# A one-token transformer block over a long key/value cache: four value slots per matmul, tiles ordered by head group, weights in longer runs and the MLP weights last

## The chip, the cores and the metric

The kernel runs on one core of one Trainium2 chip. The metric is the time of one execution on the device in microseconds (us); the number given for a kernel is the median of several executions. A profile of one execution stands beside it. It has the span, that is the time from the first to the last event on the core, and every instruction and every transfer with its start and its duration.

A core has five engines that run their own instruction streams and wait for each other with semaphores: PE (TensorE, matrix multiplication; the load of the stationary operand is shown separately as PEld), DVE (VectorE), ACT (ScalarE), POOL (GpSimd) and SP (SyncE, which here only issues transfers). Sixteen DMA engines move data from the chip's memory (HBM) to the on-chip memory (SBUF). The PE accumulates in PSUM.

## What is computed

Four batch rows, one new token each, width D = 512. With `mod = silu(c) @ w_mod` cut into six parts of width 512 (sa, ca, ga, sb, cb, gb):

```python
h = _layernorm(x) * (1 + ca) + sa
x = x + ga * attention(h)          # 32 heads, 4096 cached keys, 128 per head
h = _layernorm(x) * (1 + cb) + sb
x = x + gb * mlp(h)
```

The attention multiplies h by wq (512 x 4096), scores the query of each head against that head's 4096 cached keys, takes the softmax, sums the 4096 cached values with these weights, and multiplies the 4096 results by wo (4096 x 512). The cache is read, not written: 4 x 32 x 4096 x 128 bf16 numbers each for keys and values, 134.2 MB each. The MLP is a gated one: `z = gelu(h @ w_in)` (512 x 1792), its second half is normalised, scaled by a scalar w_sp and shifted by a scalar b_sp, multiplied with the first half, and multiplied by w_out (896 x 512). With one token per row, each cached number is used once, so there is no reuse for a matrix engine to gain from.

## The kernel before, in words

**Tiles.** The work is cut into NT = 32 tiles. A tile is one batch row and four heads: 4 x 4096 keys, laid out as 128 partitions x 128 slots x 128 numbers (partition p holds 128 consecutive key positions of head p // 32). So K of a tile is one 4 MB transfer in which each partition receives one run of 32 KB, and V likewise. Tile i is batch row i // 8 and head group i % 8.

**Buffers and order of transfers.** Two buffers for K (`kt`) and two for V (`vt`). All large transfers are issued by SP, in program order, and SP waits at each for its buffer to come free. Order: the first 1 MB of w_mod (`wmA`, L94), wq (L96), K of tiles 0 and 1, V of tile 0, the other 2 MB of w_mod (`wmB`, L123). Then in iteration i: K of tile i + 2 (L109) when the PE has finished with K of tile i, and V of tile i (L117) when the PE has finished with V of tile i - 2. In iteration 2 wo is loaded (L448) into the room that wq and w_mod leave, in iteration 4 w_in and w_out (L451, L453). V of the last tile (31) is cut into four pieces of 64, 32, 16 and 16 slots (`TAIL`). It has to wait for the V buffer that tile 29 uses.

**One iteration** (loop over i, from `QPLAN` on; the order on each engine is the order written there, nothing reorders it). For tile i: DVE multiplies K in place by the queries in two halves (`mult`, L276); the PE adds up the products over d with identity matmuls (`reduce_d`, L282, 16 per half); DVE adds the last eight (`sum8`, L291). For tile i - 1: the row maxima on DVE and the exponentials on ACT, which are written into a 128 x 128 x 4 tile `pbd` that has one nonzero column in each block of four (`scores`, L300 to L314), and the sums (`norm_r`, `norm_a`). For tile i - 2: the value product (`pv`, L340): one matmul for each of the 128 slots, with the 128 x 4 block of `pbd` as stationary operand and the 128 x 128 values of the slot as moving operand. The four column groups of the array (`tile_position`) take the slots in turn, into a PSUM tile of 128 x 128. ACT copies it out (`o_out`, L347). For tile i - 3: a matmul that adds the four groups and turns the result (`o_cols`, L352), the division by the sum (`o_scale`), and the product with the 4 x 128 rows of wo of this head group, 16 matmuls (`o_proj`, L366), which DVE adds to the accumulator (`o_add`, L374). Part of the MLP's first product, that of the sb term, is done in iteration 6 (`zbp`, L459).

**The end**, after the loop: `scores` of tile 31; `pv`, `o_cols` and `o_proj` of tile 30; the second layer norm for all rows without tile 31; then for tile 31 a value product the other way round, 128 matmuls with V as stationary operand (L537), so that the pieces can be used as they land; `o_scale`, `o_proj`, a correction of the layer norm for the last batch row; w_in (56 matmuls, L561), gelu, w_out (two times 28 matmuls, L603) and the output.

Of the kernel before, what the change touches and what calls it, by code (L numbers as in the profile page):

```python
# [8 lines left out]
BF16 = mybir.dt.bfloat16  # L9
# [6 lines left out]
HQ = 4  # L16
# [6 lines left out]
def kernel(  # L23
# [16 lines left out]

# [12 lines left out]
    R = P // HQ  # L55
    assert DH == P and R == 32 and NJ % KC == 0 and KC * RD == 512 and sum(TAIL) == NJ
    att_scale = float(DH) ** -0.5
    LN_EPS = 1e-5
    GC = 2.0 * 0.7978845608028654
# [14 lines left out]
    def ps_q():  # L74
# [8 lines left out]
    wsp_t = consts.tile([P, 1], BF16, name="wsp_t")  # L83
    bsp_t = consts.tile([P, 1], BF16, name="bsp_t")
    nc.gpsimd.dma_start(out=wsp_t, in_=B_w_sp[0:1, 0:1].to_broadcast((P, 1)))
    nc.gpsimd.dma_start(
        out=bsp_t, in_=B_b_sp.rearrange("(a b) -> a b", b=1).to_broadcast((P, 1))
    )
# [3 lines left out]
    wmod_v = w_mod.rearrange("(j p) n -> p j n", p=P)  # L92
    wmA = pre.tile([P, DJ, 2 * D], BF16, name="wmA")
    nc.sync.dma_start(out=wmA, in_=wmod_v[:, :, 0:2 * D])  # L94
    wq_sb = pre.tile([P, DJ, H * DH], BF16, name="wq_sb")
    nc.sync.dma_start(out=wq_sb, in_=A_wq.rearrange("(j p) n -> p j n", p=P))  # L96
    wmB = pre.tile([P, DJ, 4 * D], BF16, name="wmB")

    def kv_view(cache, i):
        b, g = divmod(i, NQ)  # L100
        v = cache[b, g * HQ:(g + 1) * HQ].rearrange("h s d -> (h s) d")
        return v.rearrange("(p n) d -> p n d", p=P)

    kts, vts = {}, {}

    def load_k(i):
        if i < NT:
            kts[i] = kvp.tile([P, NJ, DH], BF16, name="kt", bufs=2)
            nc.sync.dma_start(out=kts[i], in_=kv_view(A_k_cache, i))  # L109

    def load_v(i):
        if i < NT:
            vts[i] = kvp.tile([P, NJ, DH], BF16, name="vt", bufs=2)
            v = kv_view(A_v_cache, i)
            n0 = 0
            for n in TAIL if i == NT - 1 else (NJ,):
                nc.sync.dma_start(out=vts[i][:, n0:n0 + n, :], in_=v[:, n0:n0 + n, :])  # L117
                n0 += n
# [4 lines left out]
    nc.sync.dma_start(out=wmB, in_=wmod_v[:, :, 2 * D:6 * D])  # L123

# [7 lines left out]
    eps = consts.tile([P, 1], F32, name="eps")  # L132
    nc.vector.memset(eps, LN_EPS)
# [3 lines left out]
    nc.vector.memset(inv_f, 1.0 / FH)  # L137
    st2 = consts.tile([P, 2, DJ + 1], F32, name="st2")
# [7 lines left out]
    for q in range(HQ):  # L146
        nc.vector.memset(mask4[R * q:R * (q + 1), q:q + 1], 1.0)
    sel4 = consts.tile([P, HQ], F32, name="sel4")
    nc.vector.tensor_reduce(
# [523 lines left out]
```

## Time and profile before

| | |
|---|---|
| median of 3 executions | 687.23 us (686.74 to 687.46) |
| profiled execution: own time | 686.22 us |
| profiled execution: span | 684.4 us |
| read from HBM | 282.73 MB, 413 GB/s over the span |
| PE busy | 402.3 us (59%), 6574 matmuls and 6574 weight loads |
| DVE busy | 376.3 us (55%) |
| ACT busy | 93.4 us (14%) |
| mean granted PE clock | 0.805 of full |
| packets of the transfers | 16955, of these 6272 under 2 KB |

The counts of packets by size in the page include the smaller ones: 6272 under 2 KB are 1272 under 512 B and 5000 above. Bytes on the transfer queues are given in the page by queue: q1 is the hardware queue of SP's transfers, q8 carries instructions.

A profile is read from the whole to the part: first which resource is busy all the time (the table of 40 slices), then the chain of waits that ends last, then single groups of instructions and what ended the idle time ahead of them, then the timeline at the two ends of the program, where the steady pattern does not hold.

### The profile page before, as it was taken

How to read it: one execution, taken by the hardware profiler on the slowest of the kernel's cores; microseconds unless marked ns; L12 is line 12 of the kernel's file. 1: busy time of each engine (PE TensorE's matmuls, PEld its weight loads, DVE VectorE, ACT ScalarE, POOL GpSimd, SP SyncE). 2: the span in 40 equal slices, each digit the busy share in tenths (PEclk: the TensorE clock that was granted, in tenths of full speed). 3: DMA queues.
4: the chain of work that ended last, by engine and by line, in shares of the span. 5: the costliest groups of instructions: out<-in, count | busy, mean ns of one | idle time of the engine just before them, and what ended most of it. 6: DMA issues, size and time to landing. Idle time of an engine off the chain costs nothing.

```text
span 684.4 us, 14205 instructions
## 1 busy us (share of the span) xinstructions
PE 402.3 (59%) x6574; PEld 229.5 (34%) x6574; DVE 376.3 (55%) x486; ACT 93.4 (14%) x310; POOL 4.5 (1%) x17
## 2 busy tenths in 40 slices
PE   2193854844765545566745556765555566655565
PEld 2142523523332223333313333332233333323345
DVE  3383582761566645555665555556655554666542
ACT  1020211110111110111111101111110011111112
POOL 2000000000000000000000000000000000000000
PEclk9997875978788877788877887788887787788895
DMA  8999999999999999999999999999999999999971
GB/s 338 428 426 428 425 415 420 439 409 435 435 436 425 428 434 426 430 432 434 432 430 431 429 430 427 428 429 430 428 429 432 430 427 436 432 428 426 435 309 60
DMA packets 16955, 283.64 MB, mean 414 GB/s; under 512 B 1272, under 2 KB 6272, under 8 KB 8064
## 3 DMA queue, kind: packets, MB, share of 16 engines
q1 hardware_dynamic: 16800, 282.73, 96.9%
q8 instruction: 51, 0.84, 0.5%
q14 instruction: 8, 0.07, 0.0%
q0 software_dynamic: 64, 0.00, 0.0%
q10 hardware_dynamic: 32, 0.01, 0.0%
HBM read 282.73 MB, written 0.00 MB: 413 GB/s over the span
## 4 chain that ended last, share of the span: by engine, by line
DMA 60%; DVE 20%; PE 18%; SPq 1%; issue 0%; ACT 0%; DVEq 0%
DMA kt<-in_A_k_cache_dram 59%; DVE kt L276 17%; PE red L282 16%; DMA vt<-in_A_v_cache_dram 2%; DVE S L291 1%; PE ops L340 1%; PE qps L261 0%; DVE mrow L300 0%; SPq L117 0%; DVE mt L304 0%; DVE nM L306 0%; DVE mb L302 0%; PE qps L561 0%; DVE nM L307 0%; PE sm L486 0%
## 5 line engine op out<-in xcount | busy, mean ns | idle before, releaser
L282 PE MATMUL red<-kt,ident_bf 128*128 128x512 bf16 x1024 | 293.5, 451 | 235.6 <-DVE kt L276 235.5
L276 DVE TENSOR_TENSOR kt<-kt,qbc 128x8192 bf16<-128x8192 bf16 x64 | 282.9, 4421 | 236.1 <-DMA kt<-in_A_k_cache_dram 236.1
L282 PEld LDWEIGHTS <-ident_bf 128*128 128x128 bf16 x1024 | 116.4, 114 | 393.9 <-issue 228.4
L314 ACT ACTIVATE pbd<-S,nM 32x128 bf16<-32x128 f32 x128 | 73.8, 577 | 255.1 <-DVE nM L307 253.5
L340 PE MATMUL ops<-vt,pbd 128*4 128x128 bf16 x3968 | 63.4, 222 | 3.3 <-issue 3.3
L340 PEld LDWEIGHTS <-pbd 128*4 128x4 bf16 x3968 | 56.6, 86 | 4.8 <-issue 4.2
L291 DVE TENSOR_REDUCE S<-red 128x64 f32<-128x512 f32 x64 | 43.7, 683 | 4.0 <-PE red L282 3.9
L347 ACT COPY osb<-ops 128x128 f32<-128x128 f32 x31 | 8.2, 265 | 263.7 <-PE ops L340 263.7
L314 ACT ACTIVATION_READ_ACCUMULATOR pbd<-S,nM 32x1 f32 x128 | 32.1, 251 | 0.0
L366 PE MATMUL sm<-oTs,wo_sb 128*128 128x1 bf16 x512 | 17.3, 163 | 15.2 <-DMA wo_sb<-in_A_wo_dram 14.7
L366 PEld LDWEIGHTS <-wo_sb 128*128 128x128 bf16 x512 | 17.9, 101 | 15.4 <-DMA wo_sb<-in_A_wo_dram 14.7
L329 PEld LDWEIGHTS sm<-rsb,ones_f 128*128 128x128 f32 x64 | 12.1, 190 | 6.8 <-DVE acc L374 2.3
L352 PEld LDWEIGHTS sm<-sel,osb 128*128 128x128 f32 x62 | 11.6, 190 | 5.4 <-ACT osb L347 1.2
L261 PE MATMUL qps<-wq_sb,hTb 128*32 128x128 bf16 x512 | 9.4, 231 | 5.8 <-DMA wq_sb<-in_A_wq_dram 5.1
L374 DVE TENSOR_TENSOR acc<-acc,sm 128x4 f32<-128x4 f32 x31 | 4.2, 135 | 12.7 <-PE sm L366 12.7
L266 ACT CAST qbc<-qps 128x512 bf16<-128x512 f32 x8 | 4.7, 585 | 46.3 <-PE qps L261 46.3
L261 PEld LDWEIGHTS <-hTb 128*32 128x32 bf16 x512 | 8.1, 103 | 7.6 <-issue 6.6
L329 PE MATMUL sm<-rsb,ones_f 128*128 128x4 f32 x64 | 9.1, 212 | 2.3 <-DVE acc L374 2.3
L357 DVE TENSOR_TENSOR oTs<-sm,rz 128x4 bf16<-128x4 f32 x32 | 5.1, 158 | 8.8 <-PE sm L352 4.3
L322 DVE TENSOR_SCALAR rsb<-mask,rs 128x4 f32<-128x4 f32 x32 | 7.2, 224 | 4.9 <-ACT pbd L314 4.9
L300 DVE TENSOR_REDUCE mrow<-S 128x1 f32<-128x128 f32 x32 | 9.2, 286 | 1.1
L352 PE MATMUL sm<-sel,osb 128*128 128x4 f32 x62 | 8.9, 214 | 0.9 <-ACT osb L347 0.9
(132 smaller groups left out, 91.2 us busy)
## 6 DMA issues: line engine op xcount, KB each, us to landing
kt<-in_A_k_cache_dram SPq DMA_DIRECT2D x32, 4096.0 KB
vt<-in_A_v_cache_dram SPq DMA_DIRECT2D x31, 4096.0 KB, 31.9
wq_sb<-in_A_wq_dram SPq DMA_DIRECT2D x1, 4096.0 KB
wo_sb<-in_A_wo_dram SPq DMA_DIRECT2D x1, 4096.0 KB
wmB<-in_w_mod_dram SPq DMA_DIRECT2D x1, 2048.0 KB, 49.1
vt<-in_A_v_cache_dram SPq DMA_DIRECT2D x1, 2048.0 KB, 8.5
win_sb<-in_B_w_in_dram SPq DMA_DIRECT2D x1, 1792.0 KB
wmA<-in_w_mod_dram SPq DMA_DIRECT2D x1, 1024.0 KB, 5.4
```

Of the source, the lines that this page charges most:

```text
L261: nc.tensor.matmul(qp[R * q:R * (q + 1), gi, :], lhsT=hTb[:, k, b, :], rhs=wq_sb[:, k, h * DH:(h + 1) * DH], start=(k == 0), stop=(k == DJ ...
L276: nc.vector.tensor_tensor(out=kt, in0=kt, in1=bc(qbc[:, i, :], KC), op=ALU.mult)
L282: nc.tensor.matmul(red, lhsT=ident_bf, rhs=kt[:, :, m * RD:(m + 1) * RD], start=(m == 0), stop=(m == DH // RD - 1),)
L291: nc.vector.tensor_reduce(out=st[i, "S"][:, kc * KC:(kc + 1) * KC], in_=st.pop((i, "red", kc)), axis=AX.X, op=ALU.add,)
L300: nc.vector.tensor_reduce(out=mrow, in_=S, axis=AX.X, op=ALU.max)
L314: nc.scalar.activation(out=pbd[r, :, q], in_=S[r, :], func=AF.Exp, bias=nM[r, :], scale=att_scale, accum_out=rs[r, :],)
L322: nc.vector.tensor_scalar(out=rsb, in0=mask4, scalar1=st.pop((i, "rs")), scalar2=None, op0=ALU.mult)
L329: nc.tensor.matmul(z, lhsT=ones_f, rhs=st.pop((i, "rsb")), start=True, stop=True)
L340: nc.tensor.matmul(opss[i % 2][g:g + HQ, :], lhsT=pbds[i % 3][:, n, :], rhs=vts[i][:, n, :], start=(n < 4), stop=(n >= NJ - 4), tile_posit ...
L347: nc.scalar.copy(out=osb, in_=opss[i % 2])
L352: nc.tensor.matmul(op, lhsT=st.pop((i, "osb")), rhs=sel4, start=True, stop=True)
L366: nc.tensor.matmul(wp[:, j:j + 1], lhsT=wo_sb[:, g * HQ + q, j * P:(j + 1) * P], rhs=oT[:, q:q + 1], start=(q == 0), stop=(q == HQ - 1),)
```

## The change

1. **Values.** `pv` takes four slots per matmul: 32 matmuls per tile with a 128 x 16 block of `pbd` as stationary operand and 4 x 128 = 512 values as moving operand. The PSUM tile becomes 128 x 512, and only the blocks where the slot of the weights equals the slot of the values are wanted. DVE picks them with four operations and the mask `selg` (`o_pick`), in place of ACT's copy; it does so one iteration later than ACT did.
2. **Order of tiles.** Tile i is head group i // 4 and batch row i % 4. After four tiles a head group is complete, and `o_proj` runs once per group with four columns (16 matmuls per four tiles). The last group is done in two parts, three rows and one.
3. **Weights in longer runs.** w_mod is loaded whole (3 MB) as the first transfer, one run of 24 KB per partition; wq in one run of 32 KB per partition, w_in in one of 14 KB; wo of the first seven groups in runs of 2 KB. A partition now holds other rows of a matrix than before, so columns are taken with a step of four (`j:D:DJ`), also where they are loaded as stationary operand. `queries` uses 16 matmuls of 512 columns where there were 64 of 128.
4. **MLP weights last.** w_in and w_out are issued in iteration 30, behind V of tile 31, not in iteration 4. The sb term is no longer computed ahead; it rides as four further columns in the w_in product.
5. **Last tile.** V of tile 31 goes into a K buffer, the one that K of tile 30 leaves, and is issued in iteration 30. K of tile 31 is loaded in two halves.
6. Small things: w_sp and b_sp come in by two 2-byte transfers in iteration 2 in place of two broadcast ones at the start; the first layer norm uses one matmul where it used four; the turn of x at the end uses 16 small matmuls in place of four and is read from PSUM in place of through ACT; the last additions are ordered otherwise.

```diff
-    wmA = pre.tile([P, DJ, 2 * D], BF16, name="wmA")
-    nc.sync.dma_start(out=wmA, in_=wmod_v[:, :, 0:2 * D])
+    wm_sb = pre.tile([P, DJ, 6 * D], BF16, name="wm_sb")
+    nc.sync.dma_start(out=wm_sb, in_=w_mod.rearrange("(p j) n -> p j n", p=P))
...
-    nc.sync.dma_start(out=wq_sb, in_=A_wq.rearrange("(j p) n -> p j n", p=P))
+    nc.sync.dma_start(out=wq_sb, in_=A_wq.rearrange("(p j) n -> p j n", p=P))
...
-        b, g = divmod(i, NQ)
+        g, b = divmod(i, B)
...
-            nc.sync.dma_start(out=kts[i], in_=kv_view(A_k_cache, i))
+            load(kts[i], kv_view(A_k_cache, i), (KC, NJ - KC) if i == L else (NJ,))
...
+        vts[i] = kvp.tile([P, NJ, DH], BF16, name="kt" if i == L else "vt", bufs=2)
+        load(vts[i], kv_view(A_v_cache, i), TAIL if i == L else (NJ,))
...
-    nc.sync.dma_start(out=wmB, in_=wmod_v[:, :, 2 * D:6 * D])
...
-        for n in range(n0, n1):
-            g = R * (n % 4)
+        for m in range(NJ // G):
+            n = slice(m * G, (m + 1) * G)
+            g = R * (m % 4)
             nc.tensor.matmul(
-                opss[i % 2][g:g + HQ, :], lhsT=pbds[i % 3][:, n, :], rhs=vts[i][:, n, :],
-                start=(n < 4), stop=(n >= NJ - 4), tile_position=(0, g),
+                opss[i % 2][g:g + G * HQ], lhsT=pbds[i % 3][:, n, :], rhs=vts[i][:, n, :],
+                start=(m < 4), stop=(m >= NJ // G - 4), tile_position=(0, g),
             )
...
-        nc.scalar.copy(out=osb, in_=opss[i % 2])
+        nc.vector.tensor_scalar(
+            out=osb, in0=ops[:, 0, :], scalar1=selg[:, 0:1], scalar2=None, op0=ALU.mult
+        )
+        for g in range(1, G):
+            nc.vector.scalar_tensor_tensor(
+                out=osb, in0=ops[:, g, :], scalar=selg[:, g:g + 1], in1=osb,
+                op0=ALU.mult, op1=ALU.add,
+            )
...
-                    wp[:, j:j + 1], lhsT=wo_sb[:, g * HQ + q, j * P:(j + 1) * P],
-                    rhs=oT[:, q:q + 1], start=(q == 0), stop=(q == HQ - 1),
+                    wp[:, j, :], lhsT=w[:, j:D:DJ], rhs=oTs[:, g * B + b0:g * B + b1, r, t],
+                    start=(q == 0), stop=(q == HQ - 1),
...
-        elif i >= 2:
+        elif 2 <= i < L:
             load_v(i)
...
-            nc.sync.dma_start(out=wo_sb, in_=A_wo.rearrange("(j p) n -> p j n", p=P))
+            nc.sync.dma_start(
+                out=wo_sb, in_=A_wo[0:hl].rearrange("(t p r) n -> p t r n", p=P, r=2)
+            )
+            nc.sync.dma_start(out=wo_last, in_=A_wo[hl:H * DH].rearrange("(q p) n -> p q n", p=P))
-        if i == 4:
...
+        if i == L - 1:
+            load_v(L)
             win_sb = wts.tile([P, DJ, F], BF16, name="win_sb")
-            nc.sync.dma_start(out=win_sb, in_=B_w_in.rearrange("(j p) n -> p j n", p=P))
+            nc.sync.dma_start(out=win_sb, in_=B_w_in.rearrange("(p j) n -> p j n", p=P))
             wout_sb = wts.tile([P, NH, D], BF16, name="wout_sb")
             nc.sync.dma_start(out=wout_sb, in_=B_w_out.rearrange("(j p) n -> p j n", p=P))
-        if i == 6:
...
```

## The prediction, made before the changed kernel ran

> **What bounds the kernel now.** I read the 40 slices first, then the transfer queues, then the chain that ended last.
>
> ```profile
> DMA  8999999999999999999999999999999999999971
> GB/s 338 428 426 428 425 415 420 439 409 435 435 436 425 428 434 426 430 432 434 432 430 431 429 430 427 428 429 430 428 429 432 430 427 436 432 428 426 435 309 60
> DMA packets 16955, 283.64 MB, mean 414 GB/s; under 512 B 1272, under 2 KB 6272, under 8 KB 8064
> ...
> q1 hardware_dynamic: 16800, 282.73, 96.9%
> q8 instruction: 51, 0.84, 0.5%
> ...
> DMA kt<-in_A_k_cache_dram 59%; DVE kt L276 17%; PE red L282 16%; DMA vt<-in_A_v_cache_dram 2%; DVE S L291 1%; PE ops L340 1%; PE qps L261 0%; DVE mrow L300 0%; SPq L117 0%; DVE mt L304 0%; DVE nM L306 0%; DVE mb L302 0%; PE qps L561 0%; DVE nM L307 0%; PE sm L486 0%
> ```
>
> The transfers are at 9 tenths from the second slice to the 38th, at some 430 GB/s. The chain names DVE and PE too, but it only follows a K buffer round: a K transfer issued at 616.43 landed 24.6 us later, of which 9.7 us are its own 4.19 MB at 430 GB/s; the other 15 us are queue ahead of it. So a tile's compute may be some 15 us later before a transfer starts late. In the loop DVE (55% busy) and PE (59%) have room; what counts is the bytes, the rate, the head and the end. The stretches show the end:
>
> ```profile
> 101.00:112.00 11.00, 0.00 (x0) 0.00 (x0) 0.00 (x0) 0.00 (x0) 0.00 (x0) 0.50 1.13 413
> ...
> 600.00:640.00 40.00, 23.41 (x360) 12.89 (x360) 22.69 (x26) 5.16 (x18) 0.00 (x0) 0.83 1.00 430
> ...
> 650.00:661.00 11.00, 7.61 (x172) 5.07 (x171) 5.73 (x20) 2.56 (x9) 0.00 (x0) 1.00 0.65 263
> 661.00:672.00 11.00, 7.87 (x289) 7.25 (x290) 1.99 (x12) 0.77 (x3) 0.00 (x0) 0.74 0.79 326
> ```
>
> The last two numbers of a row are the DMA share and GB/s. From 650 to 661 us a third of the transfer time is empty. The timeline says why:
>
> ```profile
> 641.05 4.43 DVE L276 TENSOR_TENSOR kt<-kt,qbc 128x8192 bf16<-128x8192 bf16 x1 [8.09 <-DMA kt<-in_A_k_cache_dram]
> ...
> 655.85 1.96 PE L340 MATMUL ops<-vt,pbd 128*4 128x128 bf16 x128
> ...
> 657.85 3.11 SPq L117 DMA_DIRECT2D vt<-in_A_v_cache_dram  x4
> ...
> 661.59 1.96 PE L340 MATMUL ops<-vt,pbd 128*4 128x128 bf16 x128
> ...
> 671.74 0.59 PE L537 MATMUL sm<-pbd,vt 128*128 128x4 bf16 x16 [0.66 <-DMA vt<-in_A_v_cache_dram]
> ...
> 674.92 1.64 PE L561 MATMUL qps<-hc,win_sb 128*128 128x4 bf16 x56 [0.53 <-DVE hc L554]
> ...
> 678.31 0.94 PE L603 MATMUL red<-wout_sb,z1w 128*32 128x128 bf16 x28
> ```
>
> K31 has landed at 641.05 (call this T). V31 is issued only at 657.85, when the value product of tile 29 has freed its buffer; its last piece lands at 671.7, and 12.7 us of serial work follow.
>
> **Why not all engines run dry at 650.** In the trace's packet records each transfer ends with 16 small packets, one per DMA engine. Around K31 three engines end at 640.2 to 640.3, the other 13 at 632.0 to 635.7. A transfer counts when its slowest engine is done, so three engines, some 8 us behind, set T. What puts them behind: each of the 51 q8 packets is followed by a hole. The engine's 32 KB packets otherwise follow each other every 1.214 us; at a q8 packet there is about 1.05 us of nothing and the next packet takes about 0.5 us longer, 1.5 us together. And I take q8 for PE's instructions: its 0.84 MB over PE's 6574 + 6574 instructions is 64 B each, 256 to a packet, and the other engines run a few hundred each. An engine 8 us behind has had about five more of these than the others.
>
> **The change, part by part, up to T.** Packet times on one engine, medians of the records: 32 KB 1.214 us, 8 KB 0.309, 4 KB 0.159, 3.5 KB 0.140, 2 KB 0.086, 1 KB 0.046. That is 27 bytes per ns for the long and 22 for the 1 KB ones.
> - *MLP weights behind V31:* 512 x 0.140/16 + 896 x 0.046/16 = 4.5 + 2.6 = **7.05 us** less ahead of T (by bytes at 430 GB/s, 6.4).
> - *Head.* Before, w_mod's first part and wq were in at 17.3 and K0 at 28.4, and wmB came later: 512 x 0.159/16 = 5.1; in all 33.5. After: first bytes at 2.3 (the 2 to 3 us stretch moves 133 GB/s), w_mod 128 x 0.91/16 = 7.3, wq and K0 9.7 each, 0.8 to land: 29.8. **-3.6 us.** Of that some 1.5 is the hole from 6 to 7 us (74 GB/s) between the first two transfers; if it stays, -2.1. Next late would be K2's issue: K0's landing plus the same 15.4 us as before (28.37 to 43.72) is 45.2; the queue holds K1 and V0 until 48.7, and an issue takes about 1.6 us to the first byte (0.74 to 2.3). Covered by 2 us; if not, up to 2 us of loss.
> - *wo:* 4096 x 0.046/16 = 11.8 becomes 1792 x 0.086/16 + 512 x 0.046/16 = 11.1: **-0.7** (0 to -1.4). *K31 in halves:* 16 KB packets took 0.623, so 8 x (1.246 - 1.214) = **+0.25**.
> - *Fewer PE instructions.* Matmuls and loads: `pv` falls from 256 to 64 per tile (31 tiles: -5952), `queries` from 1024 to 256, `o_proj` from 1024 to 288, `zb` by 112; `o_cols` and the last turn of x add some 400. 13148 becomes about 6000, so 51 packets become 23. If each engine's share shrinks alike, the three engines' 7.6 us that I count ahead of T as lag (K0 to K31 and V0 to V28, 61 x 9.71 = 592.3, weights at the packet times 36.6, start and first hole 3.8: 632.7; seen 640.3) become 3.3: **-4.3 us**. Nothing in this trace shows a run with fewer: bounds 0 and -6.5 (the lag all but one hole).
> - *DVE.* `o_pick` per tile: one operation like L634 on a 128x128 PSUM tile (0.29) and three like L631 (0.36) = 1.4 us, and a reciprocal more; ACT's copy (0.27) goes. DVE does 11.3 us per 20 us now, so 12.6 after: hidden by the 15 us of queue. The same holds for `pv`: 32 x 512 columns are the 128 x 128 columns of before; 1.96 us if the four column groups overlap as now.
>
> A page rule speaks against the longer runs. The Trainium skill, "DMA: Bandwidth & Descriptors", section Specifications, gives 512 B as the minimum transfer for line rate, by which 1 KB runs would already be at full rate and the wo term would be 0 and the head term only the hole. The rows above differ from it: 0.046 us per 1 KB, and the stretch 101 to 112, which is wo, has a DMA share of 1.13 and 413 GB/s.
>
> T becomes 641.05 - 7.05 - 3.6 - 0.7 + 0.25 - 4.3 = **625.7**.
>
> **From T to the end.** V31 no longer waits: its buffer is free when `reduce_d` of tile 30 ends (635.8 before, earlier than V30's issue at 638.3), so V29, V30, V31, w_in, w_out follow T without a hole: V30 at T + 19.5 = 645.2, V31 at 655.2 (its small pieces make it 10.0), w_in 659.6, w_out 662.2, each plus up to 1. Compute: scores of tile 31 were done 19.8 us after T before (660.6), where the PE's last K product took to 655.4; with the first half of K31 landing 4.9 us early they are done near T + 13, ahead of V30. So V30 starts the last chain. Before, `pv` of tile 30 to the first of the 128 tile-31 matmuls took 661.59 to 667.76 = 6.2. After: +1.1 for `o_pick` in place of the copy; +1.0 for `pv` at a slower clock (the PE has idled about 6 us; L282 shows 6.28 against 3.61 us for the same 16 matmuls, so 1.96 to 3.9; I take 3.0); +0.4 for 16 weight loads with a step of four (no such row; between the 34 ns apart of L366 and the 114 ns of L282's loads, 0 to 1.3; I take nearer to L366, the same product). 8.7: 653.9. The 128 matmuls take 3.9 (3.33 for 112): 657.8, V31 is in by then. To w_in, 672.33 to 674.92 = 2.6, plus 0.4: 660.8, w_in just in. From there 9.5 to the end as before, less 0.6, because two of the six last DVE operations no longer wait for the variance: **669.7**; w_out is used 3.4 us after w_in starts, at 664.2, and landed by 663.2.
>
> The Trainium skill, "SBUF — State Buffer", section "Door 1: The DMA port swizzle", has bf16 strides up to 8 elements free, so the 0.4 twice would be 0 by it and the end 668.9; no run here shows it yet.
>
> Span 684.4 - 669.7 = 14.7 less. The profiled execution took 686.22; 671.5 then. The median was 1.0 above the profiled one, which I add: **672.5 us**.
>
> **Rivals.**
> 1. *The instruction packets are not what holds the three engines back*, or the holes move to others: without the 4.3, 676.8; and with the first hole staying, 678.3. For it: I infer engines from phases, and the records do not name them. Against: a hole at each q8 packet.
> 2. *The tail's new work costs more* (PE cold, weights with steps several times slower, V30 late): +0.9 on `pv`, twice 0.9 on loads, 1.0 on V30: 672.5 + 3.7 = 676; with the first part of 1 also, 680.
> 3. *Slower: the four column groups stop overlapping* with 512 columns. Place: `pv`, 32 matmuls per tile at L282's 0.226 (3.61/16) to 0.39 (6.28/16) each: 7.2 to 12.5 us instead of 1.96. PE is busy 60.5 per 100 us, 11.8 per tile of 19.5; less 1.96 plus 12.5 is 22.3, above 19.5, and 31 tiles times 2.8 give about +87, 760. It decides from a `pv` of 9.6 us per tile. At 7.2 the loop hides it and the two last passes cost 10: 683, still within or under the present. Against: 128 matmuls of 219 ns each end within 1.96 us, and the positions 0, 32, 64, 96 stay.
> 4. *It does not do what it says:* w_out and the last part of wo still run in 1 KB pieces and wo in 2 KB, so little of "long runs" is there to gain; that is in the sum. If the other order of tiles reads HBM worse, 2% of 430 GB/s (13 us) would eat the gain. K and V alternate now from far apart without a dip.
>
> **Chances.** Forecast 0.58 (669 to 675.5), rival 1 0.22, rival 2 0.12, the mild form of 3 0.03, slower or the same (3 in full, or 4) 0.05, of which 0.02 within 0.2%. A difference under 0.2% (1.4 us) is about what a measurement of this kernel can't tell from none. The range is from all terms at their good end (fetches -6.5, loads 0, `pv` 1.96: 668) to rivals 1 and 2 together: 668 to 680.
>
> **What would show it.** q8 near 23 packets; no empty stretch ahead of the last transfer; K31's landing near 626 (with fetches not mattering, near 630); the last matmuls of tile 31 waiting for PE's own chain, not for V31; `pv` near 2 us per tile. Wrong if `pv` takes over 7 us, if SP issues K2 after the queue has run out near 49 us, or if the loop's rate is under 425 GB/s.

## The result, and the profile after

| | before | after |
|---|---|---|
| median | 687.34 us (686.74 to 687.46) | 675.48 us (675.37 to 675.57) |
| profiled execution: own time, span | 686.22, 684.4 us | 675.57, 673.8 us |
| mean rate over the span | 413 GB/s | 420 GB/s |
| PE matmuls, weight loads | 6574, 6574 | 2971, 2971 |
| DVE busy | 376.3 us | 422.9 us |
| K31 landed | 641.05 us | 629.2 us |

The ratio of the times is 0.9829 (95% interval 0.9809 to 0.9848). One further execution, of 1869 us, is left out of the range and of the ratio (without it the median is 675.38). The forecast was 672.5 with a range of 668 to 680: 3.0 us too low, inside the range.

The page of the kernel after: the 40 slices, the counts of packets, the transfer queues, the chain that ended last.

```profile
DMA  9999999999999999999999999999999999999993
GB/s 374 436 431 432 407 414 418 432 434 427 429 430 433 434 433 432 427 428 431 433 430 432 431 435 428 424 434 433 430 429 432 433 435 426 431 432 424 433 414 132
DMA packets 13556, 283.19 MB, mean 420 GB/s; under 512 B 1228, under 2 KB 2644, under 8 KB 4692
...
q1 hardware_dynamic: 13488, 282.73, 98.2%
q8 instruction: 23, 0.38, 0.2%
...
DMA kt<-in_A_k_cache_dram 53%; DVE kt L275 21%; PE red L281 12%; DVE osb L362 3%; DVE S L290 1%; PE ops L350 1%; DVE osb L358 1%; DVE mrow L299 1%; DVE mt L303 1%; PE sm L387 1%; DVE rz L341 1%; DVE nM L305 0%; DVE mb L301 0%; PE qps L261 0
```

The bytes are the same (282.73 MB), the rate in the loop is the same (some 430 GB/s), and the kernel is still bound by K transfers. What differs: the first slice starts faster, the 39th is nearly full (414 GB/s where it was 309), and q8 carries 23 packets where it carried 51.

The groups of the value product: `pv` on the PE before (L340) and after (L350), and the four operations of `o_pick` on DVE (busy time, then the mean of one in ns).

```profile
L340 PE MATMUL ops<-vt,pbd 128*4 128x128 bf16 x3968 | 63.4, 222 | 3.3 <-issue 3.3
...
L350 PE MATMUL ops<-vt,pbd 128*16 128x512 bf16 x992 | 60.7, 387 | 0.0
...
L362 DVE SCALAR_TENSOR_TENSOR osb<-ops,selg,osb 128x128 f32<-128x128 f32 x93 | 32.6, 351 | 3.3
...
L358 DVE TENSOR_SCALAR osb<-ops,selg 128x128 f32<-128x128 f32 x31 | 10.8, 349 | 4.0 <-PE ops L350 3.4
```

992 matmuls keep the PE busy for 60.7 us; 3968 kept it busy for 63.4 before. The mean of one went from 222 to 387 ns with four times the columns, so the four column groups still overlap. `o_pick` is 0.35 + 3 x 0.35 = 1.4 us per tile.

The stretches of the kernel after. Behind the length of a stretch stand the busy time of PE, PEld, DVE, ACT and POOL, each with its number of instructions, then the granted PE clock (1.00 is full), the DMA share and GB/s.

```profile
200.00:600.00 400.00, 247.65 (x1575) 106.95 (x1576) 266.14 (x359) 48.54 (x168) 0.00 (x0) 0.81 1.00 431
600.00:640.00 40.00, 26.15 (x177) 11.74 (x176) 28.80 (x37) 4.63 (x16) 0.00 (x0) 0.87 1.01 431
640.00:650.00 10.00, 5.74 (x58) 3.00 (x60) 3.68 (x14) 2.30 (x8) 0.00 (x0) 0.83 0.98 419
650.00:661.00 11.00, 7.36 (x148) 5.33 (x141) 3.05 (x14) 0.50 (x2) 0.00 (x0) 0.50 0.97 391
661.00:673.00 12.00, 6.62 (x196) 5.87 (x193) 4.66 (x24) 3.75 (x8) 0.00 (x0) 0.50 0.18 62
```

There is no empty stretch ahead of the last transfer any more: 650 to 661 us has a DMA share of 0.97 where it was 0.65. The granted clock says that from 650 us the PE ran at half speed (0.50).

The timeline of the kernel after, from K31 to the output (start, duration, engine; in brackets the idle time ahead and what ended it):

```profile
624.34 4.43 DVE L275 TENSOR_TENSOR kt<-kt,qbc 128x8192 bf16<-128x8192 bf16 x1 [1.77 <-DMA kt<-in_A_k_cache_dram]
...
628.38 2.01 SPq L101 DMA_DIRECT2D kt<-in_A_v_cache_dram  x4
...
648.82 3.59 PE L350 MATMUL ops<-vt,pbd 128*16 128x512 bf16 x32
...
658.29 3.55 PE L387 MATMUL sm<-pbd,kt 128*128 128x4 bf16 x128
...
664.53 1.64 PE L550 MATMUL qps<-hcs,win_sb 128*128 128x8 bf16 x56 [0.53 <-DVE hcs L543]
```

The first half of K31 has landed at 624.34; the second half, issued with it at 606.9 and 22.3 us under way, at 629.2. V31 is issued at 628.38 (657.85 before). `pv` of tile 30 runs at 648.82, and none of the matmuls behind it waits for a transfer: the brackets name DVE or nothing.

### The profile page after: what moved, and what is told of

It reads as the page before. It is cut to its first block, busy times and chain, and to the rows that moved or that the text cites. A ratio compares the mean times of both kernels' runs of the same rounds, so it can differ in the third digit from the quotient of the medians.

```text
span 673.8 us, 7156 instructions
## 1 busy us (share of the span) xinstructions
PE 405.3 (60%) x2971; PEld 182.9 (27%) x2971; DVE 422.9 (63%) x620; ACT 84.9 (13%) x278; POOL 3.3 (0%) x15
## 3 DMA queue, kind: packets, MB, share of 16 engines
q1 hardware_dynamic: 13488, 282.73, 98.2%
HBM read 282.73 MB, written 0.00 MB: 420 GB/s over the span
## 4 chain that ended last, share of the span: by engine, by line
DMA 53%; DVE 30%; PE 15%; issue 1%; ACT 0%; SPq 0%; DVEq 0%
DMA kt<-in_A_k_cache_dram 53%; DVE kt L275 21%; PE red L281 12%; DVE osb L362 3%; DVE S L290 1%; PE ops L350 1%; DVE osb L358 1%; DVE mrow L299 1%; DVE mt L303 1%; PE sm L387 1%; DVE rz L341 1%; DVE nM L305 0%; DVE mb L301 0%; PE qps L261 0%; PE sm L185 0%
## 5 line engine op out<-in xcount | busy, mean ns | idle before, releaser
L281 PE MATMUL red<-kt,ident_bf 128*128 128x512 bf16 x1024 | 303.4, 463 | 236.0 <-DVE kt L275 236.0
L350 PE MATMUL ops<-vt,pbd 128*16 128x512 bf16 x992 | 60.7, 387 | 0.0
L362 DVE SCALAR_TENSOR_TENSOR osb<-ops,selg,osb 128x128 f32<-128x128 f32 x93 | 32.6, 351 | 3.3
L350 PEld LDWEIGHTS <-pbd 128*16 128x16 bf16 x992 | 22.3, 90 | 23.2 <-issue 1.7
L261 PE MATMUL qps<-wq_sb,hTb 128*32 128x512 bf16 x128 | 9.2, 412 | 9.2 <-DMA wq_sb<-in_A_wq_dram 8.5
L358 DVE TENSOR_SCALAR osb<-ops,selg 128x128 f32<-128x128 f32 x31 | 10.8, 349 | 4.0 <-PE ops L350 3.4
L376 PEld LDWEIGHTS sm<-sel,osb 128*64 128x64 f32 x224 | 9.2, 138 | 11.9 <-issue 11.4
L376 PE MATMUL sm<-sel,osb 128*64 128x2 f32 x224 | 11.6, 205 | 0.0
L341 DVE RECIPROCAL rz<-sm 64x2 f32<-64x2 f32 x56 | 9.1, 163 | 0.4
L303 DVE STREAM_TRANSPOSE mt<-mb 128x32 f32<-128x32 f32 x32 | 6.8, 212 | 1.1
```

Source lines behind the costliest of these rows:

```text
L281: nc.tensor.matmul(red, lhsT=ident_bf, rhs=kt[:, :, m * RD:(m + 1) * RD], start=(m == 0), stop=(m == DH // RD - 1),)
L303: nc.vector.transpose(mt, mb)
L341: nc.vector.reciprocal(out=rz[h, 0, :], in_=z[h, a:HQ:2])
L350: nc.tensor.matmul(opss[i % 2][g:g + G * HQ], lhsT=pbds[i % 3][:, n, :], rhs=vts[i][:, n, :], start=(m < 4), stop=(m >= NJ // G - 4), tile ...
L358: nc.vector.tensor_scalar(out=osb, in0=ops[:, 0, :], scalar1=selg[:, 0:1], scalar2=None, op0=ALU.mult)
L362: nc.vector.scalar_tensor_tensor(out=osb, in0=ops[:, g, :], scalar=selg[:, g:g + 1], in1=osb, op0=ALU.mult, op1=ALU.add,)
```

## The experiments

The theory was the one of the prediction: the end is set by the K transfers' own queue and then by a chain of compute from V30; a transfer counts when the slowest of the sixteen engines is done; the lag of the slow engines comes from q8. The rivals are named with each run. The median of the kernel before on the same chip stands beside each.

### The steps of K in all kernels

The start of `mult(i, 0)` is a clock for the transfers wherever DVE waited for K: the line then ends with "DMA kt". That is so for tiles 6, 7 and 31 in nearly all kernels of this study, whose labels the table gives ahead of their edits. Between tile 6 and tile 7 lie, in the kernel before, w_in and w_out and nothing else that after has not. The two lines of the kernel before and the two of after:

```profile
142.53 4.43 DVE L276 TENSOR_TENSOR kt<-kt,qbc 128x8192 bf16<-128x8192 bf16 x1 [9.38 <-DMA kt<-in_A_k_cache_dram]
...
168.56 4.42 DVE L276 TENSOR_TENSOR kt<-kt,qbc 128x8192 bf16<-128x8192 bf16 x1 [3.90 <-DMA kt<-in_A_k_cache_dram]
```

```profile
140.47 4.42 DVE L275 TENSOR_TENSOR kt<-kt,qbc 128x8192 bf16<-128x8192 bf16 x1 [0.44 <-DMA kt<-in_A_k_cache_dram]
...
160.15 4.43 DVE L275 TENSOR_TENSOR kt<-kt,qbc 128x8192 bf16<-128x8192 bf16 x1 [6.55 <-DMA kt<-in_A_k_cache_dram]
```

So the time to K31 can be cut into three parts, and a fourth is from K31 to the end of the span. The last column, the spread of K31, is explained below the table.

| kernel | q8 packets | K6 | K6 to K7 | K7 to K31 | K31 to the end | spread of K31 |
|---|---|---|---|---|---|---|
| before | 51 | 142.53 | 26.03 | 472.5 | 43.4 | 9.4 |
| e1_mlp_last | 51 | 144.23 | 19.50 | 472.5 | 46.6 | 9.5 |
| e2_v31_early | 51 | 142.65 | 26.04 | 472.4 | 43.9 | 10.1 |
| e3_four_slots | 28 | 142.90 | 27.78 | 468.1 | 47.9 | 4.8 |
| e4_pad51 | 51 | not waited for | - | 473.9 | 44.7 | 10.4 |
| **after** | 23 | 140.47 | 19.68 | 469.0 | 44.6 | 5.5 |
| e11_after_again | 23 | 140.51 | 19.42 | 469.3 | 45.9 | 5.7 |
| e5_mlp_early | 23 | 140.65 | 26.37 | 469.4 | 44.1 | 5.8 |
| e6_v31_vbuf | 23 | 139.88 | 19.43 | 468.9 | 44.9 | 5.3 |
| e7_short_runs | 23 | not waited for | - | 469.2 | 45.7 | 5.5 |
| e8_head_split | 23 | 162.96 | 19.44 | 469.4 | 44.2 | 5.1 |
| e9_head_tiles | 23 | 141.06 | 19.42 | 469.4 | 44.8 | 5.3 |
| e10_warm_tail | 23 | 140.43 | 19.42 | 468.6 | 43.8 | 5.6 |

(Where K31 is loaded in halves, that is in after and all kernels made from it, 4.9 us are added to the first half's landing, as measured in after. A steady step is 19.42 us.)

Read down a column and each of three parts of the change has a place of its own. The MLP weights are the column K6 to K7: 26.0 to 26.4 with them (27.8 in e3, of which below), 19.4 to 19.7 without, so 6.4 to 7.0 us. The packets of q8 are the column K7 to K31: 472.4 to 473.9 with 51, 468.1 to 469.4 with 23 or 28. Head, wo and the first seven iterations are K6: 2.1 us earlier after than before. From before to after: -2.06 - 6.35 - 3.4 = -11.8, which is 641.05 to 629.2.

How the packets hold K back can be read more closely than the prediction did. Each transfer raises its semaphore sixteen times, which I take as once per DMA engine, and the traces keep the time of each. For K31 of the kernel before, eight of the sixteen come at 631.6 to 634.8 us and the other eight at 639.3 to 641.0. The spread of K31 is the time from the first to the last (of its second half, where it comes in halves): 9.4 to 10.4 us in the kernels with 51 packets, 4.8 to 5.8 in those with 23 or 28. The first of the sixteen comes 19.42 to 19.46 us later from tile to tile, between K7 and K31, in every kernel of the table; only the others fall behind. So neither a lower rate nor a K transfer that was issued late lengthens this step. An estimate from these numbers: between the landings of K7 and K31, 33 packets of q8 end in before, 15 in after and 40 in e4. If each costs one engine the 1.5 us that the prediction read from the packet records, and eight engines share them, the late ones lose 6.2, 2.8 and 7.5 us. The table's step is longer than 24 steady ones (466.1 us) by 6.4, 2.9 and 7.8.

### From the side of the kernel before

**e1_mlp_last**: the MLP weights behind V31, the sb term in the w_in product.

```diff
-        if i == 4:
+        if i == NT - 1:
             win_sb = wts.tile([P, DJ, F], BF16, name="win_sb")
...
-        if i == 6:
-            zb = consts.tile([P, NF, B], F32, name="zb")
...
-                zps[:, f, :], lhsT=win_sb[:, k, f * P:(f + 1) * P], rhs=hc[:, k, :],
+                zps[:, f, :], lhsT=win_sb[:, k, f * P:(f + 1) * P], rhs=hcs[:, k, :],
```

> The kernel before with one part of the change: w_in and w_out are issued behind V of tile 31, and the sb term rides in the w_in product. My theory: K31 lands 7.05 us earlier (641.05 to about 634), the value product of tile 29 and so V31's issue and landing shift with it (671.7 to 664.7), w_in lands 4.5 us behind V31 at 669.2, 1.3 us after the PE wants it (667.9), and the end is 7.05 - 1.3 = 5.8 us earlier: 680 to 681 us beside a median of 687.3. Rival: the bytes are only put elsewhere and the end waits for them in full (687). Other rival: nothing waits and all 7.05 are gained (679.3 to 680.2).

Measured: 684.72 against 686.75 us, ratio 0.9968 (0.9957 to 0.998). Only 2.0 us. K31 came 4.8 us earlier (636.23): the step K6 to K7 lost its 6.5 us, but K6 itself was 1.7 late, and then 3.2 us went again behind K31. The timeline of e1 shows where:

```profile
656.89 3.24 PE L340 MATMUL ops<-vt,pbd 128*4 128x128 bf16 x128
...
662.76 0.36 PE L366 MATMUL sm<-oTs,wo_sb 128*128 128x1 bf16 x9 [1.25 <-issue]
...
670.24 0.51 PE L528 MATMUL sm<-pbd,vt 128*128 128x4 bf16 x13 [1.12 <-issue]
```

`pv` of tile 30 took 3.24 us in place of 1.96, at a granted clock of 0.58 where the kernel before had 1.00, and twice the PE stopped in the middle of a group for 1.25 and 1.12 us with nothing to wait for but its own instructions ("issue"). Together 3.7 us. Neither stop is in the kernel before. Between the two stops lie 256 PE instructions (128 matmuls, 127 weight loads and one wait for a semaphore), as many as the prediction counts to a packet of q8, and the PE goes on 1.4 and 1.5 us after such a packet has ended (at 661.36 and 668.74). That fits a wait for the next packet of instructions. That w_in and w_out on the queue made these packets late is a guess, and not shown. A gain at K31 is not a gain at the end unless the chain behind it keeps its length. Of the 1.7 us that K6 was late, 1.4 were lost while wo was loaded:

```profile
101.00:112.00 11.00, 0.00 (x0) 0.00 (x0) 0.00 (x0) 0.00 (x0) 0.00 (x0) 0.50 1.13 364
```

The kernel before moves 413 GB/s in this stretch, with the same transfer in the same runs of 1 KB. e2 has 416 there, e3 has 369. What makes the difference I can't say.

**e2_v31_early**: V31 into a K buffer, nothing else.

```diff
-            vts[i] = kvp.tile([P, NJ, DH], BF16, name="vt", bufs=2)
+            vts[i] = kvp.tile([P, NJ, DH], BF16, name="kt" if i == NT - 1 else "vt", bufs=2)
...
+        if i == NT - 2:
+            load_v(NT - 1)
```

> The kernel before with one part of the change: V of tile 31 goes into the K buffer of tile 30 and is issued in iteration 30, so the stretch from 650 to 661 us with a third of the transfer time empty is filled. Theory of the slow engines: three engines still had V30 to move until 659.7 to 661.4, so V31 can land on them no earlier than 661.4 + 10 = 671.4, against 671.7: no more than 0.3 to 1.5 us gained, 686 to 687. Rival: the hole is a loss for all engines, 35% of 11 us = 3.9 us gained: 683.4.

Measured: 686.78 against 686.75, ratio 1.0002 (0.9993 to 1.0012). A stretch of e2:

```profile
650.00:661.00 11.00, 8.36 (x173) 5.18 (x170) 5.78 (x20) 2.56 (x9) 0.00 (x0) 0.94 0.97 409
```

and two lines of its timeline:

```profile
638.90 2.53 SPq L117 DMA_DIRECT2D kt<-in_A_v_cache_dram  x4
...
661.77 3.43 PE L340 MATMUL ops<-vt,pbd 128*4 128x128 bf16 x128
```

V31 is issued 19 us earlier and the hole of 650 to 661 us is filled (0.97 in place of 0.65), and nothing ends sooner. `pv` of tile 30 starts at 661.77, where it started at 661.59. The last piece of V31 landed at 671.71 us, where it landed at 671.69 in the kernel before. So the hole was 3.9 us of idle transfer time that set no landing: in the kernel before, eight of the sixteen engines have done their part of V30 at 651.1 to 655.1 us and the other eight only at 659.0 to 660.4. The eight that set the landing of V31 were not idle, and the others only waited for them. Even an earlier landing would have been worth little here: the compute chain had only 0.66 us to wait for V31 before, and in e2 `pv` of tile 30 took 3.43 us at a granted clock of 0.54.

**e3_four_slots**: part 1 alone (four slots per matmul, `o_pick` one iteration later).

```diff
-        for n in range(n0, n1):
-            g = R * (n % 4)
+        for m in range(NJ // G):
+            n = slice(m * G, (m + 1) * G)
+            g = R * (m % 4)
...
-        nc.scalar.copy(out=osb, in_=opss[i % 2])
+        ops = opss[i % 2]
+        nc.vector.tensor_scalar(
+            out=osb, in0=ops[:, 0, :], scalar1=selg[:, 0:1], scalar2=None, op0=ALU.mult
+        )
```

> The kernel before with one part of the change: four value slots per matmul and the pick on DVE. PE has some 6000 instructions less, so q8 falls from 51 packets to about 28. Theory of instruction transfers: the slowest engine loses 2.8 to 4.3 us less up to K31's landing (641 to 637 or 638); the pick costs 1.4 us in the chain from there to V31's issue; the end is 1.5 to 3 us earlier: 684.5 to 686. Rival: instruction packets don't set K31's landing; it stays at 641 and the pick makes the end 1.4 to 3 us later: 688.5 to 690.

Measured: 688.69 against 686.75, ratio 1.0027 (1.0017 to 1.0037): slower by 1.9 us, where I expected 1 to 3 faster. The half of the theory that concerns q8 held: 28 packets, and K7 to K31 shortened by 4.4 us. Two other things took more than that. K7 landed 2.1 us later. DVE's longer work is not the cause of most of it: the product of tile 5 did start late (at 124.52, without waiting for its transfer; 121.66 before), but K5 itself had landed at 123.5 (121.6 before), and 1.2 us of this are the lower rate while wo was loaded (369 GB/s, see e1). The rest is open. And the tail, as its timeline shows:

```profile
662.13 3.59 PE L345 MATMUL ops<-vt,pbd 128*16 128x512 bf16 x32
...
671.09 3.55 PE L552 MATMUL sm<-pbd,vt 128*128 128x4 bf16 x128
```

`pv` of tile 30 at half clock, `o_pick` (1.5 us) behind it, and the 128 matmuls of tile 31 start at 671.09, 3.3 us later than before, all at once and at the end of the compute chain. K31 to the end became 4.5 us longer. Part 1 on its own was a loss of 1.9 us, of which some 1.2 go with the rate of wo.

### From the side of the kernel after

**e4_pad51**: 143 tiny matmuls per iteration in iterations 3 to 27, which nobody reads, so that q8 is back at 51 packets.

```diff
+PADS = 143
...
+        if 3 <= i < 28:
+            dm = ps_q()
+            for k in range(PADS):
+                g = R * (k % 4)
+                nc.tensor.matmul(
+                    dm[g:g + HQ, 0:HQ], lhsT=ident_bf[:, 0:HQ], rhs=ident_bf[:, 0:HQ],
+                    start=True, stop=True, tile_position=(0, g),
+                )
```

> The changed kernel with 143 small matmuls more (4 x 4 numbers each, into an unused PSUM bank, read by nobody) in each of the iterations 3 to 27, behind the value product, where the PE waits anyway: about 7150 PE instructions more, so q8 goes from 23 packets back to about 51, and nothing else changes. Theory of instruction transfers: K31 lands 2.5 to 4.3 us later than 629.2 and the end moves with it: 678 to 680 beside the changed kernel's 675.5. Rival: instruction packets cost nothing on the path: 675.5, within 0.5.

Measured: 680.73 against 686.75, ratio 0.9908 (0.9891 to 0.9925), that is 5.2 us above after. The queue of e4:

```profile
q8 instruction: 51, 0.84, 0.5%
```

The PE is busy for 25.9 us more (431.2 against 405.3), beside the transfers; K7 to K31 went from 469.0 to 473.9, and the tail stayed (44.7 against 44.6). With e3, which has 28 packets and the transfers of the kernel before, this decides the prediction's first rival: the instruction packets do hold the transfers back. That the 25.9 us of PE work do it is ruled out by the spread: the first engine keeps its 19.46 us per tile. 28 packets of 16 KB are 0.46 MB or 1.1 us at 430 GB/s; they cost 5.2, or 0.19 us each. A packet delays one engine by some 1.5 us. A sixteenth of that would be 0.09, an eighth is 0.19: as the updates of K31 have it, the packets weigh on eight of the engines, and the last of these counts. The Trainium skill, "Runtime: NRT & Kernel Launch", section "Instruction fetch mechanics", has instructions refilled in blocks of 16 KB, which fits these packets (0.84 MB in 51), and calls the cost of a block "mostly hidden". In a kernel whose transfers are the bound it is not: the measured 5.2 us decide.

**e5_mlp_early**: w_in and w_out back into iteration 4.

```diff
         if i == L - 1:
             load_v(L)
+        if i == 4:
             win_sb = wts.tile([P, DJ, F], BF16, name="win_sb")
```

> The changed kernel with one part undone: w_in and w_out are issued in iteration 4 again. Theory: the end follows K31's landing through the chain of compute behind it (624.34 for the first half, 673.8 for the end), and 2.75 MB ahead of K31 put it 4.8 us (what e1 showed) to 7.05 us (packet times) later: 680.3 to 682.5 us beside 675.5. Rival: the end is set by the last byte on the queue, whose sum is the same in either order, and then w_out no longer is that last byte: 674 to 676.

Measured: 683.34 against 686.81, ratio 0.9953 (0.9936 to 0.9969), 7.9 us above after. The two K steps around the weights, from the timeline of e5:

```profile
140.65 4.43 DVE L275 TENSOR_TENSOR kt<-kt,qbc 128x8192 bf16<-128x8192 bf16 x1 [0.43 <-DMA kt<-in_A_k_cache_dram]
...
167.02 4.42 DVE L275 TENSOR_TENSOR kt<-kt,qbc 128x8192 bf16<-128x8192 bf16 x1 [13.23 <-DMA kt<-in_A_k_cache_dram]
```

26.37 us from tile to tile, against 19.42. All of it arrives at the end, so the transfers behind K31 are hidden: what lies ahead of K31 is paid in full and what lies behind it is free as long as the chain behind K31 is longer. The rival, that only the last byte counts, would have given no difference.

**e6_v31_vbuf**: V31 back into the V buffer, so issued only when `pv` of tile 29 is done.

```diff
-        vts[i] = kvp.tile([P, NJ, DH], BF16, name="kt" if i == L else "vt", bufs=2)
+        vts[i] = kvp.tile([P, NJ, DH], BF16, name="vt", bufs=2)
...
-        elif 2 <= i < L:
+        elif 2 <= i:
...
-        if i == L - 1:
-            load_v(L)
+        if i == L:
```

> The changed kernel with one part undone: V31 goes into a V buffer, so it is issued behind the value product of tile 29 (643.6 instead of 628.4), and w_in and w_out behind it. Theory of the slow engines: they are at V30 until 648.8 and have the issue in time, only the fast ones run dry for some 2 us: 675.5 to 676.2. Rival: the wait is worth what the prediction filled, a hole of 2 to 4 us on the path: 677.5 to 679.5.

Measured: 675.91 against 686.81, ratio 0.9841 (0.9826 to 0.9855): 0.4 us above after, within its scatter. One line of its timeline is of use for the tail:

```profile
648.14 3.59 PE L350 MATMUL ops<-vt,pbd 128*16 128x512 bf16 x32 [0.16 <-DMA vt<-in_A_v_cache_dram]
```

`pv` of tile 30 waits 0.16 us for V30: transfer and compute arrive together. With e2 this is the second answer to the same question, from the other side: part 5 of the change is worth nothing that can be measured.

**e7_short_runs**: w_mod and wq in 14 transfers whose runs are 1 KB.

```diff
-    nc.sync.dma_start(out=wm_sb, in_=w_mod.rearrange("(p j) n -> p j n", p=P))
+    wm_v = w_mod.rearrange("(p j) n -> p j n", p=P)
+    for n in range(0, 6 * D, 512):
+        nc.sync.dma_start(out=wm_sb[:, :, n:n + 512], in_=wm_v[:, :, n:n + 512])
...
-    nc.sync.dma_start(out=wq_sb, in_=A_wq.rearrange("(p j) n -> p j n", p=P))
+    wq_r = A_wq.rearrange("(p j) n -> p j n", p=P)
+    for n in range(0, H * DH, 512):
+        nc.sync.dma_start(out=wq_sb[:, :, n:n + 512], in_=wq_r[:, :, n:n + 512])
```

> The changed kernel with w_mod and wq loaded into the same places in runs of 1 KB (14 transfers of 512 columns in place of two). By the packet times of before: 3072 x 0.046/16 = 8.8 in place of 7.3, 4096 x 0.046/16 = 11.8 in place of 9.7, so all after it is 3.6 us later: 679.1. Rival: runs of 1 KB are as fast as long ones: 675.5, plus up to 0.5 for the 12 further transfers.

Measured: 680.73 against 686.81, ratio 0.9909 (0.9894 to 0.9923), 5.2 us above after. Its stretches while the 1 KB runs are under way:

```profile
10.00:15.00 5.00, 1.17 (x31) 1.11 (x31) 0.07 (x1) 0.00 (x0) 0.00 (x0) 1.00 1.09 350
...
25.00:30.00 5.00, 0.00 (x0) 0.00 (x0) 0.00 (x0) 0.00 (x0) 0.00 (x0) 1.00 1.01 433
```

The engines are busy all the time and move 350 GB/s with 1 KB, 433 with 32 KB. K0 landed 5.0 us later (35.43), and 4.4 of these are still there at K31. The edit changes the number of transfers too, 14 for 2, and no run separates that from the length of the runs. The Trainium skill, "DMA: Bandwidth & Descriptors", section Specifications, names 512 B as the least transfer for line rate; here 1 KB is at four fifths of what 32 KB reach, and the measurement decides.

**e8_head_split**: w_mod in two transfers, as before, but into one tile.

```diff
-    nc.sync.dma_start(out=wm_sb, in_=w_mod.rearrange("(p j) n -> p j n", p=P))
+    wm_v = w_mod.rearrange("(p j) n -> p j n", p=P)
+    nc.sync.dma_start(out=wm_sb[:, :, 0:2 * D], in_=wm_v[:, :, 0:2 * D])
...
     load_v(0)
+    nc.sync.dma_start(out=wm_sb[:, :, 2 * D:6 * D], in_=wm_v[:, :, 2 * D:6 * D])
```

> The changed kernel with w_mod in two transfers as before: the third that the queries need first (2 KB runs), the rest behind V0 (4 KB runs). By packet times 2.75 + 5.1 - 7.3 = 0.55 us more, and up to 1.5 more if the hole at 6 to 7 us comes back: 676.0 to 677.6. Rival: the order at the head is worth nothing: 675.5 within 0.4. K0 lands 2 us earlier in either case (28.4 instead of 30.4), which is not on the path.

Measured: 697.97 against 686.81, ratio 1.0163 (1.0148 to 1.0178). This run doesn't answer its question. The first products waited 41.59 us for the whole tile, so for the second transfer too, which stands behind V0 and landed at 50.28. SP's line and a stretch:

```profile
70.14 0.34 SPq L102 DMA_DIRECT2D kt<-in_A_k_cache_dram  x1
```

```profile
60.00:80.00 20.00, 17.86 (x107) 6.92 (x106) 15.58 (x12) 4.09 (x11) 0.00 (x0) 1.00 0.46 185
```

K2 is issued at 70.14, 25.0 us later than in after (45.10), and the queue runs dry: 185 GB/s. The time is 22.5 us longer. If all of the lateness beyond the cover of K2's issue is paid in full, the difference, 2.5 us, is that cover, which the prediction had put at 2 us.

**e9_head_tiles**: the same question, with two tiles.

```diff
-    wm_sb = pre.tile([P, DJ, 6 * D], BF16, name="wm_sb")
-    nc.sync.dma_start(out=wm_sb, in_=w_mod.rearrange("(p j) n -> p j n", p=P))
+    wmA = pre.tile([P, DJ, 2 * D], BF16, name="wmA")
+    nc.sync.dma_start(out=wmA, in_=wm_v[:, :, 0:2 * D])
+    wmB = pre.tile([P, DJ, 4 * D], BF16, name="wmB")
...
     load_v(0)
+    nc.sync.dma_start(out=wmB, in_=wm_v[:, :, 2 * D:6 * D])
```

> The changed kernel with w_mod in two tiles and two transfers: the third that the queries need first (2 KB runs), the rest behind V0 (4 KB runs); now each product waits only for its own part. Theory from the start times of the K tiles: one transfer at the head gained 1.6 to 1.7 us at K2 (62.35 to 60.75) and kept it, so undoing it costs that: 677.0 to 677.4. The prediction's term, 3.6, less what the longer runs of wq keep: 678.5 to 679. Rival: nothing, 675.5.

Measured: 675.89 against 686.65, ratio 0.9842 (0.9829 to 0.9855); after on the same chip (e11) 675.47. K0 came 4.2 us earlier than there (26.09 against 30.29), K6 0.6 us later. Loading w_mod whole and first is worth nothing measurable; what is worth something at the head, by e7, is not to cut the weights into 14 transfers with runs of 1 KB.

**e10_warm_tail** and **e11_after_again**: the pick of tile 29 ahead of the row sums of tile 31, and 14 + 6 matmuls that nobody reads, to keep the PE's clock up; and after unchanged, on the same chip.

```diff
+    def warm(n):
+        w = ps_q()
+        for k in range(n):
+            nc.tensor.matmul(
+                w, lhsT=ident_bf, rhs=pbds[(L - 2) % 3].rearrange("p n q -> p (n q)"),
+                start=True, stop=True,
+            )
...
-    norm_r(L)
...
+    norm_r(L)
+    warm(14)
...
+    warm(6)
```

> The changed kernel with a shorter chain at the end: the pick of tile 29 goes ahead of the row sums of tile 31, and 14 and 6 matmuls without a reader (128 x 512, into an unused bank) keep the PE busy ahead of and behind the value product of tile 30, which ran at half clock (3.59 us for 32 matmuls against 1.90). If only the chain of compute behind K31's first half sets the end, up to 3 us are gained: 672.3 to 674. If the transfers are level with it (V30 lands with the start of that value product, w_out 1.1 us ahead of its use), no more than 1.1 us: 674.4 to 675.5.

> The changed kernel as it is, on the same chip as the two runs beside it: 675.5 within 0.7 us by both theories; it is there to compare with.

Measured: e10 674.85 against 686.65, ratio 0.9825 (0.9808 to 0.9842); e11 675.47, ratio 0.9836 (0.9822 to 0.9849). The 0.6 us between them are not separable. Two lines of the timeline of e10:

```profile
648.68 1.90 PE L350 MATMUL ops<-vt,pbd 128*16 128x512 bf16 x32 [1.15 <-DMA vt<-in_A_v_cache_dram]
...
662.93 1.66 PE L560 MATMUL qps<-hcs,win_sb 128*128 128x8 bf16 x56 [1.22 <-DMA win_sb<-in_B_w_in_dram]
```

The edit did what it should: `pv` of tile 30 took 1.90 us in place of 3.59. But now it waits 1.15 us for V30, and the w_in product 1.22 us for its weights. The tail of after is balanced: its compute was late by little more than the transfers are, and whoever shortens the one meets the other.

## Why the prediction was right, point by point

**The sum.** The forecast span was 669.7, the measured one 673.8. Of the 4.1 us, 3.5 are K31 (625.7 against 629.2) and 0.6 the tail. Against these the 1.0 us that I added for the median above the profiled execution did not come (675.48 against 675.57), so the time was off by 3.0. That one miss made up for a quarter of the other is luck.

- *MLP weights behind V31: right.* -7.05 forecast; -6.35 in the step K6 to K7 (6.4 by bytes was the better guide), 6.95 in e5.
- *Fewer PE instructions: right, and rather too small.* The forecast of -4.3 for the whole way is -3.3 for the 24 of 31 tiles from K7 to K31; measured -3.4. Taken out alone (e4) the term is 5.2 us. It was my least certain one, and it came from the packet records: count the holes, see which engines set the landing. One reading in it was wrong. The prediction has three engines behind at K31 and 13 ahead; the updates show eight and eight. Its packet times (640.2 to 640.3 and 632.0 to 635.7) stand 1.4 us later than the trace has them (638.8 to 638.9 and 630.7 to 634.3), so that five engines that end K31 at 640.4 to 640.6 fell out of its count. The size of the lag came out much the same: the spread of K31 falls from 9.4 to 5.5 us.
- *Head and wo: the term that failed.* "-3.6 us" and "-0.7", and some 1.0 of the fetches for these iterations, make -5.3 at K6; measured -2.06. At K2 the gain was 1.6 (62.35 to 60.75). K0 landed at 30.47, not 29.8; and from K0 to K2 after took 30.3 us for three transfers of 9.71, so 1.2 more than the sum of its parts, which the forecast did not have: K1 and K2 landed 9.71 us behind the transfer ahead of them, but V0 10.93 behind K1 (51.02 after 40.09), on one late engine, and a packet of q8 lies at 43 us. From K2 to K6 almost nothing was added (-0.45), so wo's longer runs gave no gain that shows. I had quoted the row that says so: 101 to 112 us with 1 KB runs has 413 GB/s at a DMA share of 1.13. Over 1 means that packet times overlap, and a sum of packet times then overstates the cost; 413 against 430 GB/s on 4.19 MB is 0.4 us, not the 2 by which the packet times put 1 KB above 32 KB. In e1 and e3 wo at 1 KB did cost 1.4 and 1.2 us more, at the same share of the transfer time (1.13 and 1.14); after has 414 GB/s there. Of the two values given for the head, -3.6 and -2.1, the second was the nearer.
- *K31 in halves (+0.25)*: too small to be seen. By the median of the 128 packets of 16 KB in before, 0.611 us, it would be 0.06.
- *DVE hidden by the queue*: right in after (K7 to K31 shows no trace of `o_pick`), and in e3, whose K7 to K31 is 468.1.
- *K2's issue*: forecast 45.2, measured 45.10; cover 2 us, from e8 2.5.
- *From T to the end*: forecast 44.0, measured 44.6. V30 was forecast at T + 19.5 = 648.7 with the true T; it landed at 648.62, and `pv` of tile 30 started at 648.82. From there to the 128 matmuls 9.5 us, forecast 8.7: `pv` at half clock took 3.59 in place of 3.0; the strided weight loads cost 0.1 (16 matmuls of `o_proj` 0.65 to 0.67 us, 0.54 to 0.57 before) in place of 0.4. That is near the rule that the prediction weighed, of the Trainium skill, "SBUF — State Buffer", section "Door 1: The DMA port swizzle". "So V30 starts the last chain" was only half true: the chain of the last scores ended at the same moment, with the PE at a granted clock of 0.69 during the last `reduce_d` (5.18 us against 3.61 at full clock); e6 and e10 show how close the two are.

**The rivals.** The time lies at 675.5, nearer to rival 1's 676.8 than to the forecast, and K31 at 629.2, nearer to its "near 630" than to 626. By the landmarks that I had named, rival 1 would have been taken for true. e4 shows that it is false. The landmark was badly chosen, since every term of the sum moves K31; the step K7 to K31, which only one term touches, tells them apart. Rival 2 holds with 0.6 of its 3.7 us. Rival 3 is refuted: `pv` takes 1.90 us at full clock. Of rival 4 the part on wo was true for after, and the other order of tiles cost nothing (431 GB/s from 200 to 600 us).

**The empty stretch.** The prediction read the hole of 650 to 661 us as an effect of the slow engines and gave no gain for filling it by itself. e2 and e6 bear that out, and e2 shows the cause: V31 landed at the same time (671.71 and 671.69). It is the most visible fault in the profile of before, and worth nothing.

**What the parts are worth together.** Taken out of after one at a time, the MLP weights are 7.9 us (e5) and the PE instructions 5.2 (e4): 13.1, where the whole change is 11.9. The rest of the change together therefore gave nothing or cost up to some 1 us; with medians that differ by 0.4 us for like kernels (675.47 to 675.91) I don't read more into that.

**Open.** Why the same transfer of wo ran at 413 GB/s in before and at 364 in e1; why the PE's clock at the tail differs between kernels (for `pv` of tile 30 it was 1.00 in before and e10, 0.50 to 0.58 in after, e1, e2, e3 and e6); which eight DMA engines fetch the instructions (the records do not name engines); and at which tile a packet next meets the last engine: single K steps are up to 1.1 us longer than 19.42 in after and up to 1.7 in the kernels with 51 packets, at other tiles in each run (K7 to K8 took 20.44 us in after's profile, 19.42 in e11's).

## What to carry to other kernels

In a kernel bound by one stream of transfers, take the steps of that stream from buffer to buffer and price each edit in the one step that it alone touches; a landing at the end carries all of them and tells none apart. Move what the last compute does not need at once behind the last large transfer, and count PE instructions as transfers, which delay some of the DMA engines, and so every landing. An idle stretch of the transfer engines is a gain only if something waits for its end: ask which engine's last packet releases the next instruction.

## What the runs showed of the hardware that was not expected

- 28 packets of instructions more (0.46 MB) cost 5.2 us, five times their bytes (e4). With 51 packets eight of the sixteen completions of K31 came 4 to 5 us behind the other eight (before, e1, e2, e4).
- Runs of 1 KB per partition ran at 350 GB/s in 14 transfers, and 32 KB at 433, with all engines busy in both (e7). One transfer in runs of 1 KB, wo, had 413 GB/s in before and 364 in e1.
- A DMA share above 1 (1.13 in before and in e1 at 101 to 112 us, 1.09 in e7) means that packet times overlap: the rates were 413, 364 and 350 GB/s, so the share says nothing of what is moved.
- The PE stopped for 1.25 and 1.12 us in the middle of groups of matmuls near the end of e1, with no wait that the profile shows, 256 PE instructions apart; neither before nor after has such a stop there.
- In this program a wait for a tile that two transfers fill was a wait for both, even if only the first one's part is read: it made K2's issue 25.0 us later (e8); with two tiles it did not (e9).
